# A fused attention, expert and mixing kernel: float32 projection weights split by one scaled pass on VectorE, and new order tables

## The chip, the cores and the metric

The kernel runs on one core of one Trainium2 chip. A core has five engines with queues of their own: TensorE (PE in the profile, its weight loads PEld), VectorE (DVE), ScalarE (ACT), GpSimd (POOL) and SyncE (SP), which here issues the DMAs. Each engine takes its instructions strictly in the order of its queue. The metric is the device time of one execution in microseconds, from the median of several runs.

## The reference, cut to what matters

Three stages follow one another on B = 2 batches of S = 768 rows. All arithmetic is float32.

```python
# 1. attention with 8 heads of 64; a key counts for a query only in the same hash bucket
q_bits = (einsum('bhsd,dk->bhsk', q, proj) > 0); k_bits = ...   # 6 bits each
scores = where(q_bucket == k_bucket, q @ k.T / 8, -1e9)
attn = softmax(scores) @ v
# 2. four causal attention experts, the best two of them weighted by a gate
logits = x @ w_gate; top 2; w = softmax of the two
for e in range(4):
    ye = causal_softmax((x @ wq[e]) @ (x @ wk[e]).T / 8) @ (x @ wv[e]) @ wo[e]
    out += w_e * ye
# 3. channel mixing with the row before
xk = mu_k * x + (1 - mu_k) * x_prev;  xr = mu_r * x + (1 - mu_r) * x_prev
out = sigmoid(xr @ w_r) * (relu(xk @ w_k) ** 2 @ w_v)
```

## The kernel before

The 1536 rows are twelve tiles of 128 (i = 0 to 11, six of each batch). A tile runs through three groups of steps: `lsh_steps` (per head h: `score`, a softmax, then `pv`, the product with the values), `moe_steps` (projections qk and v, per expert a causal softmax, the output projection o) and `mix_steps` (h, r and v: hidden layer, gate, down projection).

Nearly every matmul works on float16 pairs: a float32 array is split into a high part (`hi_part`, a scaled cast to float16) and a low part (`lo_part`, scaled value minus high part), and three products of the parts are summed. For a softmax this is a chain over all engines: the score matmul `s` on PE; on DVE one pass that scales and takes the minimum (P); on ACT the exponential; a high part on ACT or POOL and the low part on POOL (PHL); a DMA transpose from SP (PT); then `pv` on PE. The sixteen heads of tiles 0 and 1 (`F32T`) go another way: PE transposes the float32 P (tp), ACT or DVE copies it (PF), and `pv` is a float32 matmul, so POOL has no part in them.

The weights of stage 2 come in eight pieces through `split_w`: four of `WQK` (queries and keys), two of `WVG` (values and gate) and two of `WO`. Each piece is loaded into a float32 tile `w32` (named w_qk, w_v and w_o in the profile), multiplied in place by its scale (`nc.gpsimd.tensor_scalar`), cast to its high part, and its low part is made by `lo_part("p", ...)` on POOL. The weights of stage 3 come through `split_d` and are not touched.

The code does not issue instructions as it reads. It records operations (class `Program`; all of them then carry line 226 in the profile), and three tables at the end set what happens: `ORDER` is one order over all operations, from which every engine's queue follows, `HOMES` assigns buffers, and `ENGINES` may move a high part or a copy to ACT, DVE or POOL, whatever the letter in its call says. So "a" in `hi_part("a", ...)` is only a default: in this kernel ENGINES puts six of the eight weight high parts on POOL and two on ACT, and of the eight scalings in place seven on POOL and one on ACT.

Of the kernel before, what the change touches and what calls it, by code (L numbers as in the profile page):

```python
# [1001 lines left out]
cH5fY0kM_<TO4|IZJAvF^AV=a#uuuA0B-m%3E`xgQ9FU@+YClU#2%&CQ_kZV1%$wftn4&9$<QZn@jwR=BjjwomSdLkd3>3i=;@rF)1m{Z_s2WBY&nFj(zk`E)*x&*>}q
HEslC@Y&r>|G=mB8(l^}8}9hQZj&qN|MhqMTDRG)fQr7dp97ctWk1DDbz9tc*y`4~tNx02(AoXuhq(2wik}PD{0o1}zxOMlliTKA`rE#a|Jm2|LtS}(=(jt8$9^i*^Eu
rUzr#K96JVCx=@>rxU2Y;wg5B<%n+Nk@0i1Ui+$XOv4W`3Icgf{)4gD%;=PtVj{=0ANfAa{9Ji!(ByT9r_`)1x?GQ9Fr;Hz)$zxdQR17<=KKi#c{Z~hN|%{BEN0ABl%@
QaTKqhLM!?f>+n;e&tR#=tCy1lL^}j0|b<FTV}a;|;d~Ho_W6hudL?-gIl>mWu#UU<dr_XSkW}t<QjOe0$g1kA-p2!e_*OzP0b;-}#*oAQNta&2ZcG^)3A_=<hRQE8p2
ig{-&`w!i@2*6)Tpu8Z3W?R*yO=DYZ=J{vBAb&v!1z;Y<<2Kw&4hi~tD`nzs1EP<TZ#%IS4elOf}z5F1b3-`fNhz5^vKSYNDxC~yogOD5ZU|uYU`LGbifHK$|%VG<R39
%p!l*8E2(HFz=m>&z{WM2U*;$T0-AA<YtF}B3G5D$vuP~QrlVF`SK!+a+n9}YkzEP^F*wj1t8_yq7ApJHV!iiaT!q=BC>A&m4#AUl*o)Ew|Lj`CUIwL1#gpfw(YoNydQ
`xlrVGQcZ*iAmr!{)#m*EhK{zFvh2Y(wGQ-!8Ujj#`?DS9dkiqsD(A~KYW98+*~)48eo0Q2wff0FRmH>z;5nWH__*Y<d6v(;v3fpiQYO#<NY{4!F#HWnPC>iqbk@K&q9
1k0qrm)B!%|a0iU@uz%<EM#nX@q9y*{?&;*;}pLh;t(*>B~XZUG;j-T$Q`nkRu&hzIXALNC(R2@@89n24TV79M|&)r2xK+!27{e_7r2L0sb&^(Gsm!KXNfUEGcd*KQ~A
t((0;!J-XBGBLX(misY@UeU1x?pE40ukvgcEr2z)Lnz3Pz>f%DYyY2up|i0@=6P+6W)Y(cncO%akveODKSOxA8`>S4n|#Z8NJ8fummijGSCgX<6?gq7W&e#oUT9*?1`V  # L1010
TEZl=?@DDEXOZ-wwP355~^uoS)m8wH;?1vAa3RHll{&$S%|G*UV1<OH2_==I}le<Qd{4&4XNA{6vg^xl5F&4$9r%(eb!B0>bwrN}IgWoVJ9j9k-A5Ktz9DqqEP&7J6QT
#)A1fSg?jOu@eleB_bK|8xnU)*z8NiX0roTsm@IkbSdl$2URYdAo0C?)NpZ|)R*cNeG)+<~@mnhw%SNJh!29jy1{FVZUd7j6*yR3!cqZS?E>2A_t~QaVZ)(o+U{0=sFG
-$GkyFs`GFGz>TUthB|?#NoKr*MUrwh35O4^a}oRL+}u(Hy`{?9f}orJ-voAl$qW@O~^sNz&1KeM`#3&#8FrqM&lm(6~^E#T1`3WovQ`e=x;X;_tHLk3-6#VWT!^Z7#8
>s?xXw1t)Zhd1^;!I={?kg-=GQn=l0VEdO%HKEltJx&;T03c3SCwhl>0MG=ux}h~B%6G#_W-D!<yV@xQr0VXfam?csMf4L6b34zQCx!XNHWHy$_B2lxwq{6F*$=`nSLP
B5HjV+Go-onbn*<OR48|IeOB|2G_?+eG?=p3($dgt_PnRil4k3x0yL^aUnjUaCmBsS@3xyVM2l(f@(PuHY~~J)_T1fV#mqC`fbgITfNG(29SevG^78P*Hk8Gq5|f=DD~
SC*do4N%L?iBIcvXSd0qOa%{&ZxB-8M4m^T?rjcBn2$x|K{tqhCuhgF3(h@8|C8;Bqrq@)4R^Uopg^@7|uEr`<olf!^T**-}8vaIa=nwjn{-R&#A6kp+a3h}LQq+duQA
2LT8*l-arN$f`SMhuLoz~+fY;EOeGyYB6{AzAZHRuC1=k0!nZ^0Y53U9@oej{(kN?e(@;a+UY`>+}B#HzFhcj+#_+n1-x@-Nk<9k?H>@;a`@d;DI%kZV$P{zmJ$6Ys(r
# [23 lines left out]
HOMES = """
c-lQwjhdr443q5qL9*=Z!d$22XlZxbdH**&r8B+q@j;0rTe2MB`<IObEes%o(ToA6??xxns3&4^SA@gON7mWkP_&}-1V{Kl{)YV`e~?8Rfe8E~K=KXvm-a!0+KKo{|4T
c9750Zk5Set#CctJGya?Tsq9c_%`!m;I_yI2c-Cu=|#1IgO>W-7cd|uOu+j--=SH%TnWJbXkkwNxO)RDZuc(30?3!S)XOT+>8p*p_tqt>;V2n{&u59)rr_<n!bZdH_fS
#Qc?g~c;M8Q4;zWwDAOGI>H3+yZ>~t8NOm1r(=<<LIi$AM4#7ZB=EuE!m<X8e+w$%%O;=Ww`Y3HM5QtLmE)&rx&RBpt(RH$t}Rk*opS9dChiMCZ*Xhak8VGMBZAjLYj1
u63SS}I#e<z<S201YA+?AK4p)n5lrY!l9t%Je$%JjEl&$JNnO>U8Iv~D1|QW}^)2PZ+Pbr%Tw)Pp8F7)`-FMI0DK%PAP7xGvju_PYT?^c=55r|!eesLGo9ih_o{CiA!n
WS7?zhCKhL1HN)gmp_3w!#yJK8pTrW&-+O%QXWjY)nl_;mHoUsRQ|>paR8u2?xxk}uQkER2gyHv5Fl4t+Kta<wR*<cj0hKIWF63k($x`t=)FuuU#)($%dBQ8n?g9v-;f
n?3w$ZigEWyV}>a6T^&d6m1{mm}r$_u1v~zv-{5fVfz3D0lVx1oAu$ky`O#B&UV#Y{k-Oj=M9Y#F82{H@^qH9l15?BWkEAu0w%vVehswlB)@5kX4yNPVutCeCEL>l(`>
xkigv%9ebJDi51G(Mofj!&4xP3@8P$(6^h2cWU%>o6F<SAesOTZOD-x?xVr}WdWp1*Q+2?%7yxsay5~WII8+A5>q%=bx-_rfdtn=#K=GDGxXLqZ|FuGDJQ4xGI4e6{VF
PHOzW%$K6YCir0M^hcx
"""  # L1050
# [48 lines left out]
```

## Time and profile before

| | |
|---|---|
| median of 3 runs | 453.33 us (451.66 to 453.76) |
| profiled execution | 452.1 us |
| its span, first to last instruction | 450.3 us |
| mean granted TensorE clock | 0.996 |
| busy: PE, DVE, POOL, ACT | 433.4, 340.4, 321.9, 314.6 us |

The profile is one execution. The working of the prediction is made against its 452.1 us (span 450.3, and 1.8 around it); the median of the runs is 1.2 us above it. PE's busy time is that of pipelined records: a matmul that stands in the array while the next one waits for data counts as busy. So the busy share of PE overstates how much it does, and the chain of work that ended last is the better view of who holds the time in a stretch.

### The profile page before, as it was taken

How to read it: one execution, taken by the hardware profiler on the slowest of the kernel's cores; microseconds unless marked ns; L12 is line 12 of the kernel's file. 1: busy time of each engine (PE TensorE's matmuls, PEld its weight loads, DVE VectorE, ACT ScalarE, POOL GpSimd, SP SyncE). 2: the span in 40 equal slices, each digit the busy share in tenths (PEclk: the TensorE clock that was granted, in tenths of full speed). 3: DMA queues.
4: the chain of work that ended last, by engine and by line, in shares of the span. 5: the costliest groups of instructions: out<-in, count | busy, mean ns of one | idle time of the engine just before them, and what ended most of it. 6: DMA issues, size and time to landing. Idle time of an engine off the chain costs nothing.

```text
span 450.3 us, 14758 instructions
## 1 busy us (share of the span) xinstructions
PE 433.4 (96%) x6009; PEld 340.8 (76%) x6009; DVE 340.4 (76%) x914; ACT 314.6 (70%) x508; POOL 321.9 (71%) x345
## 2 busy tenths in 40 slices
PE   3999999999999999997999999999999999999997
PEld 3788988877888667687768876779679768966774
DVE  3899998999989878887877887578679676564431
ACT  5899899999796878885879575847757635550230
POOL 6915559789899958979879859799777847285020
PEclk9899999999999999999999999999999999999999
DMA  8987578999999997799979996999988975328101
GB/s 253 279 234 190 171 182 162 173 181 208 188 190 200 240 194 178 119 181 201 158 129 182 175 157 127 198 155 169 140 144 149 185 124 114 77 49 153 29 33 47
DMA packets 213428, 72.28 MB, mean 161 GB/s; under 512 B 204776, under 2 KB 209136, under 8 KB 213360
## 3 DMA queue, kind: packets, MB, share of 16 engines
q1 hardware_dynamic: 213184, 71.33, 83.4%
q8 instruction: 47, 0.77, 0.7%
q14 instruction: 21, 0.17, 0.1%
q10 hardware_dynamic: 176, 0.01, 0.0%
HBM read 22.04 MB, written 3.15 MB: 56 GB/s over the span
## 4 chain that ended last, share of the span: by engine, by line
PE 74%; POOL 9%; ACT 5%; DVE 5%; DMA 4%; issue 3%; POOLq 0%; ACTq 0%; DVEq 0%
PE x L226 12%; PE v L226 12%; PE h L226 12%; PE s L226 11%; PE qk L226 6%; PE r L226 6%; POOL PHL_m L226 4%; PE se L226 3%; PE o L226 3%; PE tp L226 2%; DMA PT_m<-PHL_m 2%; PE vg L226 2%; PE y L226 2%; ACT P L226 2%; POOL PHL L226 1%
## 5 line engine op out<-in xcount | busy, mean ns | idle before, releaser
L226 POOL TENSOR_TENSOR PHL<-P,PHL 128x768 f16<-128x768 f32 x80 | 134.0, 1686 | 16.7 <-ACT PHL L226 12.1
L226 ACT ACTIVATE P<-P,mx 128x768 f32<-128x768 f32 x96 | 88.0, 930 | 16.6 <-DVE P L226 14.4
L226 DVE TENSOR_SCALAR_CACHE_REDUCE P<-s 128x768 f32<-128x768 f32 x96 | 90.4, 950 | 10.4 <-PE s L226 5.2
L226 PE MATMUL s<-y,x 128*128 128x384 f16 x384 | 77.0, 328 | 0.8 <-DVE P L226 0.8
L226 PE MATMUL h<-mk,WK 128*128 128x128 f16 x1152 | 73.0, 219 | 0.1
L226 PEld LDWEIGHTS <-WK 128*128 128x128 f16 x1152 | 67.0, 98 | 4.6 <-issue 1.0
L226 PE MATMUL v<-WV,k2h 128*128 128x512 f16 (+1 forms) x208 | 57.7, 363 | 0.0
L226 PEld LDWEIGHTS <-x 128*128 128x128 f16 x480 | 38.6, 98 | 21.7 <-ACT x L226 3.3
L226 PEld LDWEIGHTS <-PT 128*128 128x128 f16 x1440 | 50.1, 98 | 5.9 <-issue 1.5
L226 PE MATMUL x<-vh,PT 128*128 128x65 f16 x960 | 53.4, 194 | 0.5 <-DVE xT L226 0.5
L226 PE MATMUL x<-vl,PT 128*128 128x64 f16 x480 | 39.4, 193 | 0.0
L226 POOL TENSOR_SCALAR PHL<-P 128x768 f16<-128x768 f32 x39 | 33.1, 851 | 8.3 <-ACT P L226 5.2
L226 POOL TENSOR_TENSOR PHL_m<-P_m,PHL_m 128x512 f16<-128x512 f32 (+2 forms) x24 | 33.8, 1415 | 6.6 <-ACT PHL_m L226 5.8
L226 PE MATMUL v<-WV,k2l 128*128 128x512 f16 (+1 forms) x104 | 37.7, 363 | 0.0
L226 PE MATMUL qk<-xT,WQK 128*128 128x128 f16 x576 | 37.0, 219 | 0.0
L226 ACT ACTIVATE PHL<-P 128x768 f16<-128x768 f32 x41 | 34.3, 838 | 2.3 <-PE x L226 0.7
L226 PEld LDWEIGHTS <-WQK 128*128 128x128 f16 x576 | 34.1, 98 | 2.0
L226 PE MATMUL r<-WR,mr 128*128 128x512 f16 x144 | 35.0, 379 | 0.0
L226 ACT ACTIVATE t<-h 128x512 f32<-128x512 f32 x24 | 14.2, 592 | 23.5 <-PE h L226 20.3
L226 PEld LDWEIGHTS <-k2h 128*128 128x128 f16 x208 | 18.6, 98 | 13.9 <-issue 1.0
L226 DVE SCALAR_TENSOR_TENSOR h<-h,t 128x512 f32<-128x512 f32 x24 | 16.6, 692 | 15.5 <-ACT t L226 15.5
L226 POOL TENSOR_TENSOR mk<-m32k,mk 128x512 f16<-128x512 f32 x12 | 14.2, 1185 | 17.6 <-ACT mk L226 15.9
(181 smaller groups left out, 929.5 us busy)
## 6 DMA issues: line engine op xcount, KB each, us to landing
raw_k<-in_moe_w_k_dram SPq DMA_DIRECT2D x8, 512.0 KB, 5.1
raw_v<-in_moe_w_v_dram SPq DMA_DIRECT2D x8, 512.0 KB, 4.5
q<-in_q_dram SPq DMA_DIRECT2D x12, 256.0 KB, 6.1
k<-in_k_dram SPq DMA_DIRECT2D x8, 384.0 KB, 4.2
v<-in_v_dram SPq DMA_DIRECT2D x8, 384.0 KB, 5.4
out_dram<-e SPq DMA_DIRECT2D x11, 256.0 KB, 2.7
raw_r<-in_moe_w_r_dram SPq DMA_DIRECT2D x4, 512.0 KB, 4.1
PT<-PHL SPq DMA_TRANSPOSE x80, 4.4
```

Source lines behind the costliest of these rows:

```text
L226: getattr(getattr(self.nc, engine), method)(*[real(a) for a in args], **{k: real(a) for k, a in kw.items()})
```

## The change

In `split_w` the scaling in place goes. The high part takes the scale itself, and the low part is one DVE instruction (scale times source minus high part) in place of a POOL subtraction. That is 8 scalings fewer, and 8 low parts that stand on DVE and no longer on POOL. `F32T` is as it was. All three tables are new.

```diff
-        nc.gpsimd.tensor_scalar(w32, w32, sc, 1.0, op0=OP.mult, op1=OP.mult)
-        hi_part("a", hi, w32)
-        lo_part("p", lo, w32, hi)
+        hi_part("a", hi, w32, sc)
+        lo_part("v", lo, w32, hi, sc)
...
 ORDER = """
-c-jrtg8~@F768%R>y2&Owr$(CZQHhO+qP}CK^v4w8#eF##F?q!)H&y!ICH_F0~g8Vb}?K8SKr5Vd0bvs)8%soTs#-wC2>_<85hM>a}iy2SJ35m30xsp*d=mhT~wFUC3d
+c-jrtg8~@F5&*#6yVb?EZQHhO+qP}nwr$(C(}rzQhHdlSe8m7L2vh)r0Fi)z0U<YdNC=Uk4CH~lP!_5}K8ONapga_Sa!?RzKm^DS4&p*Js1B7ODpY|TSP=@rH0Tb|pb`
...
```

The new ENGINES table also moves other high parts and copies. Counted over the program: off DVE go 4 PF, 6 copies of transposed queries (x), 2 kT, 2 qT, one each of WK, WR, WV, xT, y, yT and x2t, and three small zl; onto it come 3 vnh. Off ACT go 2 nak, 2 naq, 2 nbq, 3 vh, 2 mk, 2 hl_y, 3 vnh, a WQK and the one scaling that stood there, and it takes what left DVE besides 3 nbk. POOL takes 2 nak, 2 naq, 2 nbq, 3 vh, 2 mk, 2 hl_y and a WQK, and gives 3 nbk and a PHL_m. After the change the eight weight high parts stand on POOL (seven) and ACT (one, a WO).

Three places show the new order; behind P, s and PHL the first number is the head, behind q and nbq<-q the tile. The first is POOL's queue early in the program, behind the high part of query tile 1 (nbq<-q_1), where the first weight pieces are handled. Before:

```order
L226 TENSOR_SCALAR nbq<-q_1_238 128x8x64
L226 TENSOR_SCALAR w_qk_224<-w_qk_224 128x512
L226 MEMSET vh_0_284 128x24x2
L226 MEMSET causal 128x128
L226 AFFINE_SELECT causal<-causal 128x128
L226 TENSOR_SCALAR w_qk_332<-w_qk_332 128x512
L226 TENSOR_SCALAR WQK<-w_qk_332 128x4x128
L226 TENSOR_SCALAR WQK<-w_qk_224 128x4x128
L226 TENSOR_TENSOR WQK<-w_qk_224,WQK 128x4x128
L226 TENSOR_TENSOR WQK<-w_qk_332,WQK 128x4x128
L226 TENSOR_SCALAR nbq<-q_2_502 128x8x64
```

And the same place now:

```order
L226 TENSOR_SCALAR nbq<-q_1_148 128x8x64
L226 TENSOR_SCALAR nbk_0_1_96<-k_0_0_1_132 128x12x64
L226 TENSOR_SCALAR WQK<-w_qk_214 128x4x128
L226 MEMSET vh_1_365 128x24x2
L226 TENSOR_SCALAR nbk_0_0_200<-k_0_0_0_113 128x12x64
L226 TENSOR_SCALAR vh_0_98<-v_0_0_1_392 128x12x64
L226 TENSOR_SCALAR vh_1_365<-v_0_1_1_412 128x12x64
L226 MEMSET vnh_496 128x24x2
L226 TENSOR_SCALAR nbq<-q_2_432 128x8x64
```

Between the two query tiles POOL has one weight high part left of six weight passes, and two high parts of values (vh) have come in.

The second place is DVE's queue among the score passes (P) of tiles 0 and 1. Before:

```order
L226 TENSOR_SCALAR P_2_554,mx_391<-s_2_530 128x768
L226 TENSOR_SCALAR P_0_556,mx_391<-s_0_547 128x768
L226 SCALAR_TENSOR_TENSOR wd_k_0_552<-raw_k_0_399,wd_k_0_552 128x512
L226 TENSOR_SCALAR P_3_607,mx_608<-s_3_581 128x768
L226 SCALAR_TENSOR_TENSOR nbq<-q_2_502,nbq 128x8x64
L226 SCALAR_TENSOR_TENSOR WK_0_0_604<-wd_k_0_552,WK_0_0_604 128x512
```

And now, in front of the same low part of query tile 2 (nbq<-q_2):

```order
L226 TENSOR_SCALAR P_1_549,mx_390<-s_1_514 128x768
L226 SCALAR_TENSOR_TENSOR WK_2_512_553<-wd_k_512_536,WK_2_512_553 128x512
L226 TENSOR_SCALAR P_1_567,mx_568<-s_1_540 128x768
L226 SCALAR_TENSOR_TENSOR WQK<-w_qk_168,WQK 128x4x128
L226 SCALAR_TENSOR_TENSOR nbq<-q_2_432,nbq 128x8x64
L226 TENSOR_SCALAR P_2_600,mx_390<-s_2_561 128x768
```

A weight low part (WQK) now stands between score passes on DVE; it is the second of the eight, and six of them stand ahead of DVE's last score pass of tile 2.

The third place is POOL's queue among the PHL passes of tile 2, where the first piece of WO was handled. Before:

```order
L226 TENSOR_SCALAR PHL_2_1088<-P_2_983 128x768
L226 TENSOR_TENSOR PHL_2_1088<-P_2_983,PHL_2_1088 128x768
L226 TENSOR_SCALAR w_o_718<-w_o_718 128x512
L226 TENSOR_SCALAR PHL_5_1094<-P_5_905 128x768
L226 TENSOR_TENSOR PHL_5_1094<-P_5_905,PHL_5_1094 128x768
L226 TENSOR_SCALAR naq_1179<-q_9_771 128x8x64
L226 TENSOR_SCALAR WO<-w_o_718 128x512
L226 TENSOR_TENSOR WO<-w_o_718,WO 128x512
L226 TENSOR_TENSOR PHL_0_1141<-P_0_1121,PHL_0_1141 128x768
```

And now:

```order
L226 TENSOR_TENSOR PHL_1_1161<-P_1_1049,PHL_1_1161 128x768
L226 TENSOR_SCALAR PHL_7_1247<-P_7_1078 128x768
L226 TENSOR_TENSOR PHL_7_1247<-P_7_1078,PHL_7_1247 128x768
L226 TENSOR_TENSOR PHL_6_1153<-P_6_1103,PHL_6_1153 128x768
L226 TENSOR_SCALAR nbq_1254<-q_9_918 128x8x64
L226 TENSOR_TENSOR PHL_4_1210<-P_4_1130,PHL_4_1210 128x768
L226 TENSOR_SCALAR nbq<-q_4_926 128x8x64
L226 TENSOR_TENSOR PHL_5_1230<-P_5_1213,PHL_5_1230 128x768
```

No weight pass stands between these PHL passes any more; the one WO pass that POOL keeps comes ten instructions later, and high parts of queries (nbq) have come in.

## Rows read from the trace of the kernel before

**Rows 1.** Page, part 1: busy us, share and instructions by engine.

```profile
PE 433.4 (96%) x6009; PEld 340.8 (76%) x6009; DVE 340.4 (76%) x914; ACT 314.6 (70%) x508; POOL 321.9 (71%) x345
```

**Rows 2.** Busy time by stretch; each engine's busy us (instructions) stand in the header's order.

```profile
core 0: us, PE busy (x) PEld busy (x) DVE busy (x) ACT busy (x) POOL busy (x), PEclk, DMA share, GB/s
0.00:25.00 25.00, 17.08 (x206) 14.32 (x207) 15.85 (x41) 17.88 (x31) 18.62 (x34) 0.93 0.96 265
25.00:62.00 37.00, 37.00 (x348) 33.42 (x346) 35.54 (x75) 34.79 (x70) 15.22 (x16) 1.00 0.73 189
62.00:125.00 63.00, 60.70 (x923) 51.15 (x921) 58.70 (x175) 58.26 (x105) 55.91 (x58) 1.00 1.01 183
125.00:240.00 115.00, 111.55 (x1648) 84.37 (x1645) 96.28 (x247) 91.97 (x140) 97.03 (x97) 1.00 1.00 181
240.00:450.00 210.00, 207.03 (x2901) 157.54 (x2898) 134.06 (x379) 111.69 (x166) 135.10 (x142) 1.00 0.72 126
```

**Rows 3.** Chain that ended last, 25 to 62 us, shares by line.

```profile
by line: PE x L226 42.6%; PE s L226 24.6%; PE tp L226 21.3%; PE qk L226 5.4%; PE tr_x L226 4.8%; PE tr_y L226 0.9%; PE z_q L226 0.5%
```

**Rows 4.** The same chain, 62 to 125 us.

```profile
by line: PE x L226 17.5%; PE s L226 13.9%; POOL PHL L226 10.4%; DMA PT<-PHL 7.8%; PE qk L226 7.6%; PE tp L226 4.7%; PE h L226 4.4%; DVE P L226 3.9%; PE tr_x L226 3.7%; PE se L226 3.0%; PE vg L226 2.2%; PE o L226 2.2%; DVE xT L226 1.9%; POOL
```

**Rows 5.** Groups: PHL and the weight passes on POOL; count | busy us, mean ns | idle before.

```profile
L226 POOL TENSOR_TENSOR PHL<-P,PHL 128x768 f16<-128x768 f32 x80 | 134.0, 1686 | 16.7 <-ACT PHL L226 12.1 <-DVE y L226 1.4 <-DVE qT L226 1.1
...
L226 POOL TENSOR_TENSOR WQK<-w_qk,WQK 128x512 f16<-128x512 f32 x4 | 4.6, 1161 | 1.5 <-ACT WQK L226 1.3
...
L226 POOL TENSOR_TENSOR WVG<-w_v,WVG 128x512 f16<-128x512 f32 (+1 forms) x2 | 2.4, 1180 | 0.1
L226 POOL TENSOR_SCALAR w_qk<-w_qk 128x512 f32<-128x512 f32 x3 | 2.4, 786 | 6.4 <-DMA w_qk<-in_moe_wq_dram 6.4
L226 POOL TENSOR_TENSOR WO<-w_o,WO 128x512 f16<-128x512 f32 x2 | 2.3, 1162 | 1.5 <-ACT WO L226 1.4
...
L226 POOL TENSOR_SCALAR w_v<-w_v 128x512 f32<-128x512 f32 (+1 forms) x2 | 1.2, 625 | 0.5 <-DMA raw_k<-in_moe_w_k_dram 0.5
...
L226 POOL TENSOR_SCALAR w_o<-w_o 128x512 f32<-128x512 f32 x2 | 1.2, 620 | 0.0
```

**Rows 6.** Waits of POOL, 25 to 62 us: total us, times, longest.

```profile
POOL w_qk L226 <- DMA w_qk<-in_moe_wq_dram: 6.4, 1, 6.4
POOL WQK L226 <- ACT w_qk L226: 5.4, 1, 5.4
```

**Rows 7.** DVE low parts nbq with two operands in SBUF: ns min/median/max, first and last start.

```profile
L226 DVE SCALAR_TENSOR_TENSOR nbq<-q,nbq x8: 682/760/1179, 5.5 to 206.0; 128x512 f16<-128x512 f32 x8
```

**Rows 8.** Timeline: DVE low parts and the POOL passes beside them; start us, us.

```profile
16.95 0.69 DVE L226 SCALAR_TENSOR_TENSOR nbq<-q,nbq 128x512 f16<-128x512 f32 x1 [1.05 <-POOL nbq L226]
16.99 1.12 POOL L226 TENSOR_SCALAR w_qk<-w_qk 128x512 f32<-128x512 f32 x1
...
86.40 1.09 DVE L226 SCALAR_TENSOR_TENSOR nbq<-q,nbq 128x512 f16<-128x512 f32 x1
86.97 2.02 POOL L226 TENSOR_TENSOR PHL<-P,PHL 128x768 f16<-128x768 f32 x1
```

**Rows 9.** Groups that ENGINES moves: count | busy us, mean ns | idle before.

```profile
L226 ACT ACTIVATE PF<-tp 128x384 f32<-128x384 f32 x24 | 11.2, 495 | 0.3 <-PE tp L226 0.3
L226 ACT ACTIVATE x<-tr_x 128x512 f16<-128x512 f16 x15 | 8.4, 589 | 2.0 <-PE tr_x L226 1.8 <-DVE x L226 0.2
L226 DVE COPY x<-tr_x 128x512 f16<-128x512 f16 x17 | 6.6, 415 | 0.4 <-POOL mk L226 0.4
L226 DVE TENSOR_SCALAR PF<-tp 128x384 f32<-128x384 f32 x8 | 4.4, 552 | 0.6 <-PE tp L226 0.6
L226 ACT ACTIVATE vh<-v 128x768 f16<-128x768 f32 x5 | 4.2, 839 | 0.2 <-DMA v<-in_v_dram 0.2
L226 POOL TENSOR_SCALAR nak<-k 128x768 f16<-128x768 f32 x4 | 4.1, 1023 | 2.2 <-DMA k<-in_k_dram 1.9
L226 ACT ACTIVATE nak<-k 128x768 f16<-128x768 f32 x4 | 3.4, 839 | 2.3 <-DMA k<-in_k_dram 1.7 <-DMA PT_m<-PHL_m 0.6
```

More of the change, by code (lines that the diff above doesn't have):

```diff
@@ L1002 @@
[L1002 to L1017, printed above, removed]
@@ new lines @@
+UySkG<VJOo$0E5k|nHPzfvJC;W`1@Cv5DtJv2i!~X6A4uRwt3uE94NbJ``N*oR`F*fFcaZnOh!Uiaf{ain2YS;0LT*90<z+J}37!mJd6g-6+VI&NNj~EG8L3Y>#1#z;Q
+;*P;)nCc$kSeFqW<7yZN<6IeB18d;{zQSMeA)dw?coxsV8JqxL@Lzn5$DtFf)pOVmZsJXU0;aj!INnWncW{P#ga6?VyoD3oM0XMfx}Whqe#IpIH#`NC+*x>nm*8*w1qZ
+p)FcAj3Z}=A1xp(*-pW>hRJ3hm|a58`!4}airm)s}y=U{|O=Kn$O&cjHz+`YsUeu%pOL*06}!9B;z@DpByneGK%0dgzcN|(|vaH;$#sDf94-7JT0m`m-eVl@<Z4V+u$(
+)u)h4$OA#VU!!~()rq$!PmkXILFO}g-%_1zsOyOj6Rbe<L1F)m)Y0Ejc${B0;}D8Sf`s^9ju4ug3IFTVtt(JZuvE?h+hB=aG7h3^V|}b)o1e!v8XTRyTC$-;O4u=*cm%
@@ new lines @@
+RJG||mLL+Q~O)-jVhR>i2w!z4*Jw|uM{RVA|-EghzfZcJ6YmPbmbJ*%i_^!CkwZM*;&-cLXt|i8BFW?^J_dRh6G_&0<r;q4%xJa&mkLseid%mE*<CnTZ{;tpNce$M|iM
+#L9xCj0vOod!Nw@>aK`lN1;d*oBNy{;3+bm`q=pVr-nukyraaJ?{&OXgC#eXf+x<72ssz7_Vt-Wbo7_UT-F_tYnFsa#j+hkfz6FXK!4O1>K;bT52tSJ}sPqp^n1=q6Go
+SKn9h{jq{?>L)=WHvp^pXMVqH;19Tg*wEMXg?&9=)_?RjU=SX3ljv_h7|Z!uehA)zPyVR833+{W-^|~JL$0~M1E2kG{)nsX-}<|7*d24JT~?RbWpi0vBR>=y`)WS1JK-
+Kcc30lN^Cw*n*TjGK(Wr%g2szzIJnnM2I{v+{>%aJ~emIW6==2C0+c5ma|L(ubuRgbH<sChSQTWYIrGNZnYU%U1K%U0nG|KBD&>y~y|KR`hQ|P59`qxjvvG|jZNaOL8n
+}Dr-TmQ4q=l=4q{5ZVo?z(n<Dz^92@U)wZ)2V}>K^=WTHxbXenKX-LQvvs%|KaD+9QqCJxlVpQz4nD%es|u@r3<czn}iqL4R_5Ic1%JKTv1ov6?0`>IcF4u-uN@FxQjy
@@ new lines @@
+$Bhl{=lS;TUuB5x<fOb%1nvLh&ER0H*-A<Z`f54w`-92>o-6OZ3{(_rs4#uLtp_J?FOS=P9f{_+bH@}PK;(Uxt^Kb#~rmnt=KT8Lxr*GsMxcV+0b@%Zp3hklCu9t7<ln
+4*ea%}8+_!StN5>ON8@f<BA#&@s`pSXYImb>j1(Mn82$LKKq0|{vvohQMjZZTb;i=<e=C8i~G$2D`u=@(dqt1$^BrAqEStf6F7#U-aTc!Ew+Ww)Gug%q?FhxzGP)qQ|!
+?jwA3z5R2Sl8(??s^QkrQ}@hWaWC8qtnT{xm+lm8qSW-0``Nv6uiXHjmM&3Emx|KRUK;4v>mXl}-?;Vk)~%plTspc%OKCIx3#TaqRdgFDBMtU_{7;aceswFUzaQea(0|
+a^{{X;MG{%qh@7+eaLGRo|KgoY^*J&Xx!o@h<BmU+l`>izGucmQ+hTlfp=_cK#J2cbx=etzPEx{6$iAMO^u8#Za{&chaQvB@xa6iLF%}Rf{-`y9Noj$=gSJ%CQdhRIgq
@@ L1039 @@
+%x4=9R`Mbwm=`t6X_NDgi2P7Pugv}Z|AIUxMO#1Sa>SWWRX_3e&K;Vv`01~3<`t8xbWD9hw-6Zcw$xTsdWs`taIoeMurJtRH$lQLZ?v8x`rWPVrU;0>k?h69YVM8K|V_
+NuuOlG-{lYaQ>xo@8xVf77xvN$S|MAmE3}xc)W76!S*4%kXB!=QgfU@gcx|h-h)oK=+t^Ul-q?Ga5(?Wpn-)G=X)9yJZE7fCC9Razu$orO%Gz7|#U_X8;WztWGs3SnGt
+3IJ!)GaHbHX21-fEi<e_I{<Y=7A&qwuGFv9I>cFu3sj|H)XRbHn_wFf0xdG|USN!lJMwSXdL5g%Bcyr6FQi5$ak!t8Z&Vq_8}!4lBdD5IOu~tHS>9uN@2xY<>98HiRE`
+AnXkL0)#_hQ`i``gw0`V*cP^jBVk849HNA%AzFwYVuW2`cQ_i3h2!BwI2lfb)8R}w8!m)BVQ)AW8ru1AF<c6l!<BF~TnpF3jc_yk4@ABGj{
 """
@@ L1046 @@
[L1046 to L1049, printed above, removed]
+c-lo&4R@O`5If!Z3)_UPX~Q7tl9Y}9|9?1Ln!dpckY}GP>12yMuc!kcxj-TQGc6K)Kt-X(7eYxe3;Z&z(4;=f*_<l^1pa|G!B5x^VF`-xfmgAC6+jhv1Ad8pi2N1(4b8
@@ L1055 @@
-D{we^^r8-(xPaWi?XHwu7sjr3CjU!
+c-pO12@=F02$SUhf8KF>d4K~b)6z~W5FlbHov<oAFN*NFUO`>YsxCWBHYlADmHYl_MLjFhXy@Vsg5jAK-ZgLB$@#q1xO#28y`#noRYNNk^FVhp?yxWtl6n(l=m8C)Ow9
+_^86Rvc0MiVtvPV`aat*sAV9%6*+p##eFiw(Wn2OhD%)w|>kBvioL$&jYF*b|6XO^RkcIza?IMG{|+pwZD&c`-xj0u=a8A9TsYV6#T5NU&R5DQbL4nzFyL`ju%T;wRh=
+vZbDwq@%W`P>;PdHDf8j{%$
 """
```

62 lines of the change are left out of this document (31 added, 31 removed).

## The prediction

> **What bounds the kernel now.** I read the page's first part, then busy time by stretch, then the chain of work that ended last in each stretch, and only then single groups. By the first part TensorE is busy 433.4 of 450.3 us [rows 1], but that counts matmuls that stand waiting in the array, so the chain decides who holds the time. The stretches [rows 2] show four phases. From 0 to 25 us everything fills up: PE is busy 17.08 us, the granted clock is 0.93 on the mean, DVE, ACT and POOL have 15.85, 17.88 and 18.62. From 25 to 62 us, the float32 heads, the chain is PE alone [rows 3], yet DVE (35.54 of 37.00) and ACT (34.79) are nearly full beside it, while POOL has 15.22 and is mostly idle. From 62 to 125 us all are nearly full (DVE 58.70, ACT 58.26, POOL 55.91 of 63.00) and the chain jumps: POOL's PHL passes hold 10.4% of it, the transposes behind them 7.8%, DVE's score passes 3.9% [rows 4]. From 240 us PE has 207.03 of 210 while DVE has 134.06, ACT 111.69 and POOL 135.10: there the other engines wait for PE and nothing that the change does to them counts, unless it is moved there in bulk. So the change can win or lose between 0 and 240 us, and which engine is relieved matters only by stretch.
>
> **GpSimd's side: 14.1 us of passes go.** Low parts: 4.6 (WQK), 2.4 (WVG), 2.3 (WO); scalings in place: 2.4, 1.2, 1.2 [rows 5]; sum 14.1 us. Of this, WQK and WVG (10.6 us) lie between 17 and 50 us. From 25 to 62 us POOL stood idle for 21.8 us [rows 2], 6.4 of it waiting for the w_qk load and 5.4 for the one scaling that ACT did [rows 6], and the chain has no POOL piece there [rows 3]. Those 10.6 us are worth nothing by themselves. The WO passes, 2.3 + 1.2 = 3.5 us, and the 1.4 us for which POOL waited for ACT's WO part [rows 5], 4.9 us in all, lie in the full stretch. POOL holds there 10.4% of a chain of 63 us, 6.5 us, in its PHL passes [rows 4]; a pass less ahead of them is time only where POOL's queue, and not the exponential ahead of it, was last. Bounds: 0 and -4.9. I take -1.0, near the zero end, since the new table puts seven or eight high parts (nak, nbq, naq, vh) into POOL's queue, at 1.02 us for a nak [rows 9], so POOL's relief over the program is nearer 9 than 14 us.
>
> **VectorE's side: eight passes come.** Each is 512 columns from two operands in SBUF. The trace has no such pass on w32, but its nearest kin is the low part of the queries: same shape, same two operands in SBUF, 682 to 1179 ns, median 760 [rows 7]. Eight of them are 5.5 to 9.4 us. Six stand early, where POOL is mostly idle, so I take 0.70 for these; two (WO) stand among PHL passes, and I take 1.09 [rows 8]: 4.2 + 2.2 = 6.4 us. What leaves DVE by the tables: 4 PF at 552 and 6 copies at 415 ns [rows 9], 4.7 us; eleven others less three vnh that come, net eight at about 0.5 us as an estimate from these two rows, 4 us. Over the program DVE is some 2 us lighter. But the eight passes are all in front of 125 us, and where DVE had 1.46 us to spare from 25 to 62 us and 4.3 us from 62 to 125 us [rows 2], six early ones (4.2 us) do not fit without something leaving. Some does: the copies and PF of the float32 heads lie in this same stretch. I count what stands ahead in the tables' order at two landmarks, every instruction at its group's mean, an estimate. At DVE's last score pass of tile 5 DVE has about 2.8 us more ahead of it than before, and PE about 4.8 us more; at that of tile 8, both have about 3 us less. So the tables moved PE's work along with DVE's, and the lead of DVE over PE grows by about 1 us at its worst place. Bounds: 0 (all covered by what left) and +4 (six passes uncovered). I take +1.0.
>
> **The port that both engines use.** The row at 86.40 us shows the DVE pass at 1.09 us in place of 0.69, and POOL's pass beside it at 2.02 [rows 8] in place of 1686 ns on the mean [rows 5]; at 16.95 us DVE kept 0.69 and POOL's scaling of w_qk took 1.12 [rows 8], where 0.62 is the time of the w_v scaling [rows 5]. The Trainium skill, page "SBUF — State Buffer", section "Who interferes with whom", states that a VectorE instruction with two SBUF inputs contends with a GpSimd instruction that reads SBUF, and that the loser is fully blocked. Both rows agree with it as far as a loser goes, but the losses are 0.4 to 0.5 us, not the 1.65 us of a whole PHL pass. By the rule each of the eight passes would cost one engine up to such a wait; it speaks against the change and is priced among the rivals.
>
> **ScalarE's side.** It takes the 4 PF at 495 and the 6 copies at 589 ns, 5.5 us, and some eleven others, and gives 2 nak and 3 vh at 839 ns, 4.2 us [rows 9], and about a dozen small ones. The net is near +3 us over the program, an estimate from these rows. Between 25 and 125 us ACT was busy 34.79 + 58.26 = 93.05 of 100 us [rows 2], so what comes early can push the exponentials back. Bounds 0 (PE's work moved along, as at the landmarks above) and +2.5 (most of it early and uncovered); I take +0.5.
>
> **Start, buffers, transfers, end.** The load order at the start puts the key halves of heads 4 to 7 first and one half behind a weight block. The first score pass, which needs those heads, could come earlier; but PE's queue holds the transposes of the late half ahead of it, and the bytes in front of the last key half are the same as before. I take 0, bounds -1.5 and +1.5. The number of transposes and loads is the same, and the DMA share of 1.01 and 1.00 from 62 to 240 us [rows 2] gets no relief: 0. Behind 240 us PE's work is the same, instruction for instruction, and I take -0.5 for 62 to 240 us as a whole, where the tables carry about as much work as before but POOL's queue is some 9 us less far behind; bounds -3 and +3.
>
> **Sum.** -1.0 + 1.0 + 0.5 + 0 - 0.5 = 0. Against the profiled execution that is 452.1 us; the median of the runs is 1.2 us above it, and since the profile is one execution inside a range of 451.66 to 453.76 us I put the forecast between the two, at 452.6 us. A measurement of this kernel can tell about 0.5%, 2.3 us, from no change.
>
> **The rivals.** First, faster: POOL's queue is what holds the chain from 62 to 240 us more than the exponentials are, and the relief reaches PE. For it speaks the 10.4% of POOL in the chain, against it that POOL waited in that same stretch for ACT. Price: the 4.9 us of WO, or 3.9 with 1.0 already counted, and up to 1 to 2 us at the start: 452.6 - 4 = 448.6, at best 447. Second, slower: DVE becomes the bound between 25 and 125 us. It decides from the point at which more than the spare 1.46 us (25 to 62) is added net of what leaves; then every further us of DVE delays the score passes, the exponentials behind them, and PE's pv. Price: six early passes, 4.2 us, less 1.46, is 2.7, and ACT's 2.5 on top: 452.6 + 5 = 457.6. Third, each of the eight passes meets a POOL pass that reads SBUF, as at 86.40 us: DVE's cost goes to 8 x 1.18 = 9.4 us, 3.0 above the 6.4 counted, and where POOL loses its PHL passes grow by 0.35 us: 452.6 + 3 = 455.6. For it speaks the row at 86.40 us, against it that six passes stand where POOL is busy 15.22 of 37 us. It adds to the second. (This is how it would go by the rule of the Trainium skill's page "SBUF — State Buffer" cited above.) Fourth, the change does not do what it says on ScalarE: its high parts are put on POOL by the table (seven of eight), so ScalarE has nothing to gain; that is in the sum already and gives the forecast.
>
> **How the numbers follow.** No change that can be measured, 450.3 to 454.9 us: 0.40. Faster by the relief of POOL: 0.33. Slower by DVE or by the port, 0.27, of which 0.07 is the port alone. For the range I leave out 1 in 10 on either side: a third of the faster cases lies below the 4 us that the WO passes are worth, and a third of the slower ones above the 5 us of DVE and ACT, so 447.5 to 458.0. The likeliest case's own range is the 450.3 to 454.9 above.
>
> **What would show it.** Right: eight SCALAR_TENSOR_TENSOR on WQK, WVG and WO at 0.69 to 1.1 us on DVE; POOL's busy time down by about 9 us and DVE's by 1 to 3; DVE at 35 to 37 of 37 us and the chain still PE alone from 25 to 62 us; the stretch from 240 us unchanged. Wrong towards slower: PE idle or DVE in the chain between 25 and 62 us, the last score pass of tile 1 later by over 2 us. Wrong towards faster: POOL's PHL below 8% of the chain from 62 to 125 us and PE reaching the same matmul 3 us earlier at 125 us. The forecast fails as a whole if the tables change the coupling of the queues at places that no row here names, since a new order over all operations is more than the eight passes that I could price.

## The result

| kernel | us, median (lowest to highest) | ratio to before, 95% interval |
|---|---|---|
| before | 452.67 (451.66 to 453.76, 4 runs) | 1 |
| after | 447.19 (447.05 to 448.11, 4 runs) | 0.988 (0.985 to 0.991) |
| after, measured again beside later experiments | 447.48 (446.85 to 449.04, 6 runs) | 0.992 (0.989 to 0.995) |

The change makes the kernel 4 to 5 us faster. The forecast was 452.6 us, no change, with 447.5 as the low end of its range: wrong. The profiled execution of after took 448.11 us, with a span of 446.3.

### The profile page after: what moved, and what is told of

Same layout as the page of the kernel before. It is cut to its first block, busy times and chain, and to the rows that moved or that the text cites. A ratio compares the mean times of both kernels' runs of the same rounds, so it can differ in the third digit from the quotient of the medians.

```text
span 446.3 us, 14743 instructions
## 1 busy us (share of the span) xinstructions
PE 430.6 (97%) x6009; PEld 339.2 (76%) x6009; DVE 336.3 (75%) x901; ACT 317.1 (71%) x518; POOL 315.3 (71%) x340
## 4 chain that ended last, share of the span: by engine, by line
PE 62%; ACT 11%; POOL 9%; DVE 9%; DMA 4%; issue 4%; SPq 0%; POOLq 0%; DVEq 0%; ACTq 0%
PE v L226 11%; PE h L226 11%; PE x L226 8%; PE s L226 8%; PE r L226 6%; POOL PHL L226 5%; PE qk L226 4%; ACT P L226 3%; PE o L226 3%; DVE P L226 3%; PE y L226 2%; PE se L226 2%; PE vg L226 2%; POOL PHL_m L226 2%; DMA k<-in_k_dram 2%
## 5 line engine op out<-in xcount | busy, mean ns | idle before, releaser
L226 POOL TENSOR_TENSOR PHL_m<-P_m,PHL_m 128x512 f16<-128x512 f32 (+2 forms) x24 | 34.7, 1450 | 7.6 <-ACT PHL_m L226 6.8
L226 ACT ACTIVATE P_m<-P_m,bias_m 128x512 f32<-128x512 f32 (+2 forms) x24 | 19.6, 821 | 20.5 <-DVE P_m L226 17.9
L226 DVE SCALAR_TENSOR_TENSOR h<-h,t 128x512 f32<-128x512 f32 x24 | 16.6, 694 | 19.8 <-ACT t L226 19.7
```

Of the source, the lines that this page charges most:

```text
L226: getattr(getattr(self.nc, engine), method)(*[real(a) for a in args], **{k: real(a) for k, a in kw.items()})
```

## The profile after

Part 1 of the page of after (busy us, share, instructions; [rows 1] before):

```profile
PE 430.6 (97%) x6009; PEld 339.2 (76%) x6009; DVE 336.3 (75%) x901; ACT 317.1 (71%) x518; POOL 315.3 (71%) x340
```

POOL is 6.6 us lighter, DVE 4.1 lighter, ACT 2.5 heavier. By stretch, beside [rows 2], same columns:

```profile
0.00:25.00 25.00, 16.19 (x207) 13.39 (x208) 16.62 (x40) 18.35 (x33) 15.49 (x31) 1.00 0.99 278
25.00:62.00 37.00, 37.00 (x326) 32.84 (x324) 33.54 (x75) 36.54 (x78) 13.51 (x15) 1.00 0.75 170
62.00:125.00 63.00, 61.28 (x971) 52.16 (x969) 59.94 (x173) 57.83 (x107) 58.16 (x57) 1.00 0.99 191
125.00:240.00 115.00, 113.18 (x1714) 87.95 (x1711) 98.78 (x249) 92.79 (x138) 98.61 (x100) 1.00 0.98 186
240.00:450.00 210.00, 202.99 (x2810) 152.90 (x2806) 127.46 (x367) 111.61 (x167) 129.57 (x139) 0.99 0.69 122
```

From 25 to 62 us DVE is 2.0 us lighter, although passes on the weights were added: more left it there than came. ACT is 1.75 us heavier and has 0.46 us left. From 62 to 125 us POOL is 2.25 us **heavier**: the tables put more into its queue there than the weights took out. The chain of 62 to 125 us shows who is late there ([rows 4] before: POOL PHL 10.4%):

```profile
by line: POOL PHL L226 20.3%; issue 12.5%; DVE P L226 11.9%; ACT P L226 7.5%; POOL nbq L226 3.0%; DVE m32k L226 2.7%; POOL gt L226 2.6%; ACT P_m_p L226 2.6%; ACT PHL L226 2.6%; DVE P_m_p L226 2.5%; DVE rs L226 2.5%; ACT PF L226 2.4%; DVE m3
```

and that of 25 to 62 us, which was PE alone in [rows 3]:

```profile
by line: PE x L226 24.7%; PE s L226 19.8%; ACT P L226 19.3%; PE tp L226 14.9%; ACT PF L226 6.7%; ACT raw_r L226 3.1%; PE tr_x L226 3.0%; DVE P L226 2.6%; ACT wd_r L226 1.4%; ACT WO L226 1.4%; ACT WK L226 1.3%; ACT WR L226 1.3%; PE tr_y L226
```

The eight new passes (ns min/median/max; first and last start):

```profile
L226 DVE SCALAR_TENSOR_TENSOR WQK<-w_qk,WQK x4: 683/698/1210, 18.1 to 50.6; 128x512 f16<-128x512 f32 x4
...
L226 DVE SCALAR_TENSOR_TENSOR WVG<-w_v,WVG x2: 790/854/919, 61.6 to 67.4; 128x528 f16<-128x528 f32 x1, 128x512 f16<-128x512 f32 x1
...
L226 DVE SCALAR_TENSOR_TENSOR WO<-w_o,WO x2: 1099/1414/1730, 88.7 to 95.0; 128x512 f16<-128x512 f32 x2
```

Together 3.3 + 1.7 + 2.8 = 7.8 us. They stand later than the prediction had them: both WVG passes are at or behind 62 us.

**PE's lag** is the measure for where time goes: the time at which a matmul starts, less what all the matmuls ahead of it on PE take back to back (worked out from the step between matmuls of each shape in these traces; 414.9 us in all, the same in every kernel). It is read at equal amounts of PE work, since the orders differ:

| PE work done, us | 24 | 48 | 64 | 88 | 104 | 184 | 192 | 240 | end |
|---|---|---|---|---|---|---|---|---|---|
| before | 13.5 | 13.4 | 15.0 | 17.0 | 19.5 | 24.5 | 26.9 | 28.7 | 32.0 |
| after | 13.4 | 13.5 | 14.4 | 17.3 | 18.5 | 22.2 | 22.2 | 24.3 | 28.0 |
| new passes, old order | 13.6 | 16.2 | 18.6 | 20.8 | 23.5 | 28.7 | 29.6 | 31.3 | 34.6 |
| old passes, new order | 13.6 | 13.7 | 14.7 | 19.8 | 21.0 | 23.5 | 23.5 | 25.6 | 29.2 |
| new order, WO old | 12.8 | 12.9 | 13.8 | 19.0 | 20.2 | 23.0 | 23.0 | 25.0 | 28.6 |
| new order, only WO new | 13.4 | 13.5 | 14.5 | 17.4 | 18.5 | 21.1 | 21.2 | 23.2 | 26.8 |
| old order, only WO new | 13.4 | 13.2 | 15.6 | 17.8 | 20.5 | 25.7 | 30.0 | 31.7 | 35.0 |
| before, early query turn | 13.1 | 13.0 | 14.6 | 16.7 | 19.1 | 24.2 | 24.5 | 26.6 | 29.9 |

A row is one execution, and those of one kernel differ by 1 to 2 us (after, profiled again: 13.7 at 24, 16.3 at 64, 29.0 at the end). In that case most of it comes where the granted clock differs. Here is the stretch from 70 to 78 us in after and in after again (columns as in [rows 2]):

```profile
70.00:78.00 8.00, 7.23 (x90) 6.51 (x90) 7.86 (x19) 7.48 (x14) 6.83 (x6) 1.00 1.16 217
70.00:78.00 8.00, 7.23 (x74) 6.83 (x74) 6.36 (x15) 6.58 (x10) 6.14 (x5) 0.79 1.24 213
```

PE is busy for the same 7.23 us in both, but has 74 matmuls instead of 90 where part of the stretch ran at the lower of the clock's two levels, 1.2 instead of 2.4 GHz. The row "old order, only WO new" is affected too: it is an execution of 455.14 us (median of that kernel 453.1), with a granted clock of 0.79 on the mean from 212 to 220 us, in the stretch in which its lag rises from 25.7 to 30.0.

Between before and after nothing happens in the first 48 us of work. One us is gained by 104, 1.3 more on the way to 184, then 2.4 at once between 184 and 192, and nothing behind that.

The sudden step is a stall of the kernel before, in its timeline at 203 to 213 us (start us, us, [idle before <-releaser]):

```profile
203.57 1.23 SPq L226 DMA_TRANSPOSE x<-naq  x1
...
210.35 0.60 ACT L226 ACTIVATE t<-h 128x512 f32<-128x512 f32 x1 [2.91 <-DMA x<-naq]
...
212.34 0.58 ACT L226 ACTIVATE x<-tr_x 128x512 f16<-128x512 f16 x1
...
212.97 0.36 PE L226 MATMUL z_q<-prhl,x 128*128 128x12 f16 x8 [2.04 <-ACT x L226]
```

HOMES gives `t` of tile 3 the slot in which `naq` of tile 8 lay, and SP issued the transpose that reads `naq` only at 203.57, in its queue behind other transfers. ACT waited 2.9 us for it, the copy of `x` stood behind `t` in ACT's queue, and PE's hash of tile 7 behind that. In the tables of after the two do not meet. The weights have no part in it. How much it costs varies: with the new passes in the old order the lag rises by only 0.9 us there, from 28.7 to 29.6.

## Experiments

**The theory**: the gain belongs to the order of the work (A), in part to that one stall. **Rivals**: GpSimd's relief itself (B); the passes cost VectorE time that the order wins back (C). The further letters (A1, A2, D, E, F) are defined in the expectations that use them. Differences in microseconds are the ratio's distance from 1, times 452 us, unless something else is named; the runs stem from four chips, and each was measured beside before on its own chip.

### Passes and tables apart

```diff
 split_w as after (no scaling, low part on VectorE)
-ORDER, HOMES, ENGINES of after
+ORDER, HOMES, ENGINES of before, without the eight scalings
```

> The new way of splitting the weights (scale and round in one pass, one VectorE pass for the low part) in the order, the slots and the engines of the kernel before; the eight scalings are dropped and each low part stands where its GpSimd pass stood. Theory A (the gain is the order of the work, not the passes): 452 to 453 us, as before, and ScalarE still waits 2.9 us for the transpose of the queries at 207 to 210 us, with the 2.0 us stall of PE behind it. Theory B (GpSimd's relief is the gain): 447 to 449 us, as after. Theory C (the eight passes on VectorE cost, and the order had to win that back): 454 to 457 us.

Measured: 455.35 us, 1.007 of before (1.005 to 1.010): 3.2 us slower. C's size, and B is out for this order.

```diff
 ORDER, HOMES, ENGINES of after, each scaling put ahead of its high part
-split_w as after
+split_w as before (scaling and low part on GpSimd)
```

> The other corner: the order, slots and engines of the kernel after, but the weights split as before: eight scalings on GpSimd, each right in front of its high part, and eight low parts on GpSimd. Theory A (order): 447 to 449 us, at most 1.5 us above the kernel after. Theory B (relief of GpSimd): 451 us or more, since the 14 us of passes are back in GpSimd's queue. No stall of ScalarE at about 207 to 210 us by either, since the slots are those of after.

Measured: 449.53 us, 0.993 (0.990 to 0.996): 3.2 us faster than before without any new pass, some 2 us short of after. So the tables alone win about 3 us, and **the same passes cost 3.2 us in the old order and save 0.5 to 2 us in the new one** (0.993 against the two measurements of after, 0.988 and 0.992; with the second the intervals overlap, so the saving rests on the waits shown under the WO pieces as well).

In the old order DVE's queue around 40 us shows the cost:

```profile
39.30 0.95 DVE L226 SCALAR_TENSOR_TENSOR WQK<-w_qk,WQK 128x512 f16<-128x512 f32 x1
40.18 1.09 DVE L226 SCALAR_TENSOR_TENSOR WVG<-w_v,WVG 128x512 f16<-128x512 f32 x1
...
41.31 0.67 DVE L226 TENSOR_SCALAR rs<-sm 128x4 f32<-128x4 f32 x1
...
42.70 0.41 DVE L226 TENSOR_TENSOR x<-x,rs 128x256 f32<-128x256 f32 x1
```

and the waits of that kernel from 38 to 47 us what PE paid (total us, times, longest):

```profile
PE tp L226 <- DVE nbq L226: 0.9, 1, 0.9
...
PE x L226 <- DVE x L226: 0.7, 1, 0.7
```

Two passes stand ahead of `rs` and `x` of tile 0, for which PE waits: 2.8 us of lag by 48 us of work (16.2 against 13.4). In after they stand behind score passes (at 30.57 and 43.45 us), and PE loses nothing there.

The two halves of the tables, the order (with the slots) and the engines, were then split:

```diff
 kernel after
-ENGINES of after
+ENGINES of before for 182 operations (the weights' stay)
```

> The kernel after with the 182 operations that its engine table moved put back on the engines of the kernel before (the weights' passes stay as in after, and so do order and slots). Theory A1 (what makes room for the eight passes is the move of copies from VectorE to ScalarE): VectorE is about 2 us busier early, PE loses 1 to 3 us before 62 us of its work, 449 to 452 us. Theory A2 (where the instructions stand in the order is what counts, the engines little): 446.5 to 448.5 us.

Measured: 502.92 us, 1.113.

```diff
 new passes, ORDER and HOMES of before
-ENGINES of before
+ENGINES of after
```

> The new split of the weights and the engines of the kernel after, but the order and slots of the kernel before. Beside the run with the old engines as well (455.4 us). Theory A1 (engines make room): the 2.2 us that PE loses at 41 to 43 us there go, 450 to 453 us. Theory A2 (places count): 454 us or more, since the two passes on WQK and WVG still stand ahead of rs and x of tile 0, on which PE waits.

Measured: 498.47 us, 1.106. In the first run both theories missed by 50 us; in the second A1 missed by 45, and A2 had named no upper end. The waits of the first show queues out of step (the same two lines are 12.1 and 20.3 us in all in before):

```profile
POOL PHL L226 <- ACT PHL L226: 37.5, 14, 8.2
ACT t L226 <- PE h L226: 28.2, 13, 9.7
```

An instruction that changes its engine without changing its place stands in a queue that was not ordered for it, and whatever is behind it waits; that this is the whole of the 50 us is argued from these waits, not shown. Order and engines cannot be taken apart here, so how much each gives stays open.

### The stall at the end of the gain

```diff
 kernel before, SP's queue
+DMA_TRANSPOSE x2_8<-naq_8
 DMA_TRANSPOSE PT_m5_1<-PHL_m5_1
 dma_start v32_1_0_1
-DMA_TRANSPOSE x2_8<-naq_8
```

> The kernel before with one instruction moved: the transposing DMA of tile 8's queries goes three places earlier on SP's queue, right behind the first PT_m of tile 5, so that the slot which ScalarE's t of tile 3 takes over is free in time. Theory A (this one stall is worth 2.2 to 2.4 us of the 5.5): 450.2 to 450.6 us, and the lag of PE does not jump at z_q7. If something else is late next at the same place: 452 to 453 us. If the earlier transpose delays the PT_m behind it on the queue: above 453 us.

Measured: 450.2 us, 0.997 (0.995 to 0.999): 1.5 us faster, and the lag goes from 24.2 to 24.5 where before goes from 24.5 to 26.9. The stall is real and worth 1.5 of the 4 to 5 us (0.5 to 2.4 by the interval). (The transpose moved ahead of the two transfers shown, one place less than its expectation says.)

### The WO pieces

```diff
 kernel after
-all eight pieces split in the new way
+WQK and WVG in the new way, the two WO pieces as before
```

> The kernel after, with the two WO pieces alone split as before (scaling and low part on GpSimd, about 4 us of passes in the full stretch from 62 to 125 us); WQK and WVG as in after. With all eight pieces split as before in this order it was 449.5 us. Theory A (the relief of GpSimd counts at WO alone, -2.5 us): 449 to 450 us, with the loss at s_4 and y_1 at 103 to 107 us. Rival (the relief of the early pieces counts as well): 447.5 to 448.5 us.

Measured: 448.87 us, 0.995 (0.992 to 0.998). That is, within the intervals, the time with all eight pieces as before (449.53, 0.993): in this order the WO pieces seem to carry all that the new passes save. The interval also overlaps that of after's second measurement (0.989 to 0.995), so the trace has to decide. Where, the timeline of this kernel shows from 98 to 104 us, first POOL, then who waits for it:

```profile
98.41 1.16 POOL L226 TENSOR_TENSOR WO<-w_o,WO 128x512 f16<-128x512 f32 x1
...
99.53 2.10 POOL L226 TENSOR_TENSOR PHL<-P,PHL 128x768 f16<-128x768 f32 x1
...
101.67 0.96 DVE L226 TENSOR_SCALAR_CACHE_REDUCE P<-s 128x768 f32<-128x768 f32 x1 [1.54 <-POOL PHL L226]
...
103.40 0.60 ACT L226 ACTIVATE WR<-wd_r 128x512 f16<-128x512 f32 x1 [2.56 <-DVE rs L226]
```

In after, the same DVE pass:

```profile
102.48 0.96 DVE L226 TENSOR_SCALAR_CACHE_REDUCE P<-s 128x768 f32<-128x768 f32 x1 [0.50 <-POOL PHL L226]
```

In the new order POOL runs without a gap here, and a score pass needs the slot that POOL's low part still reads. The wait reaches PE; its waits in this kernel from 98 to 107 us:

```profile
PE y L226 <- DVE WR L226: 1.7, 1, 1.7
PE s L226 <- DVE P L226: 0.8, 1, 0.8
```

With all eight pieces as before they are 1.6 and 0.8 us; in both profiles of after, and with only the WO pieces new, the first is 0.6 us and the second is absent. Here POOL **is** last, and a pass less in its queue is time: the lag at 88 us of work is 19.0 with the old WO pieces and 17.3 without, at 104 us 20.2 and 18.5.

```diff
 kernel after
-all eight pieces split in the new way
+the two WO pieces in the new way, WQK and WVG as before
```

> The kernel after, with the six early pieces (WQK and WVG) split as before, on GpSimd, and only the two WO pieces split in the new way. Theory A (the WO pieces are the whole gain of the new passes; the six early ones cost VectorE what the prediction said, +1.0 us): 445.5 to 446.5 us, faster than after. Theory F (GpSimd's relief by the early pieces counts too, since its queue is behind from there on): 448 to 450 us.

Measured: 447.01 us, 0.991 (0.989 to 0.994), beside 447.48 for after on the same chip:

> The kernel after, unchanged, as a measure for the other three on the same chip: 446.5 to 447.5 us, 0.988 to 0.990 of before.

Both theories missed: the times are the same within the noise. So the six early pieces are worth nothing that these runs can tell in the new order, on either engine, and WO is what counts. In the old order:

```diff
 kernel before
-all eight pieces as before
+the two WO pieces in the new way, at the places of GpSimd's passes
```

> The kernel before, with the two WO pieces alone split in the new way (no scaling, low part on VectorE, at the places where GpSimd's passes stood); WQK and WVG as before. In the new order these two pieces were worth 2 to 3 us. Theory A (GpSimd's relief at WO counts in any order): 449 to 450.5 us. Theory E (in the old order VectorE's passes at 75 to 102 us cost what GpSimd's relief gives): 451.5 to 453 us.

Measured: 453.1 us, 1.005 (1.002 to 1.007): 2.1 us slower (by the medians on that chip, 453.1 and 451.7, 1.4), which is theory E. The same edit has the other sign. POOL's timeline of this kernel around 70 us:

```profile
68.16 0.62 POOL L226 TENSOR_SCALAR WO<-w_o 128x512 f16<-128x512 f32 x1
70.67 1.65 POOL L226 TENSOR_TENSOR PHL<-P,PHL 128x768 f16<-128x768 f32 x1 [1.89 <-ACT PHL L226]
```

and that of before:

```profile
69.86 1.16 POOL L226 TENSOR_TENSOR WO<-w_o,WO 128x512 f16<-128x512 f32 x1
70.97 1.65 POOL L226 TENSOR_TENSOR PHL<-P,PHL 128x768 f16<-128x768 f32 x1
```

POOL is done with WO 2.2 us earlier and then waits 1.89 us for ACT's high part: the PHL pass starts 0.3 us earlier, no more. In the old order ACT was last, and the relief turned into a wait. The 1.23 us that the pass takes on DVE stay, and PE's `vg` waits 0.6 us for the copy behind it. The second piece shows the same: POOL skips 1.16 us of WO and then waits for ACT:

```profile
99.29 1.64 POOL L226 TENSOR_TENSOR PHL_m_p<-P_m_p,PHL_m_p 128x512 f16<-128x512 f32 x1 [2.26 <-ACT PHL_m_p L226]
```

In before this pass starts at 98.76 us, in an execution that is 0.5 us ahead by then.

```diff
 kernel before, only WO new, DVE's queue
-low part of WO (first piece)
 PF of tile 1, vl, P_m_p, lg, zl_q3, z_q3
+low part of WO (first piece)
```

> The kernel before with the two WO pieces split in the new way (453.1 us, +2.1), and the first of their VectorE passes moved behind PF of tile 1, vl and the hash sum of tile 3, some 4 us later on VectorE. Theory A2 (the place of the pass): the 0.9 us that PE lost at vg_0 at 74 us go, 451.5 to 452.5 us. Theory D (VectorE's sum in this stretch): the loss comes back a few us later, 453 us or more.

Measured: 453.05 us, 1.005 (1.002 to 1.007): no gain. The 0.6 us wait went from `vg` at 74 us, and one of 0.8 us came up at `x` (tile 2) at 78.7 us. That is theory D's number, but not plainly its mechanism: the trace names a memset late in POOL's queue there, and no run takes that apart.

```diff
 kernel before
+the two WO pieces in the new way
+DMA_TRANSPOSE x2_8<-naq_8 two transfers earlier on SP, as above
```

> The kernel before with two edits by hand: the WO pieces split in the new way, and the transposing DMA of tile 8's queries three places earlier. The second alone gave 1.5 us. Theory A (the gain of after is these two things, each added to the other): 447 to 449 us, within 0.5% of the kernel after. Theory E: 450 us or more, and the rest of the gain is the new order as a whole.

Measured: 451.52 us, 1.000 (0.998 to 1.002). -1.5 and +2.1 nearly cancel. Theory A in this form (stall and WO relief, each by itself) falls: the WO relief is worth something only in an order in which POOL is last.

### The early pieces

```diff
 kernel after
 lo_part("v", lo, w32, hi, sc)
+lo_part("v", lo, w32, hi, sc)
```

> The kernel after with each of the eight low parts made twice on VectorE, the same result written again: about 7.9 us more of VectorE, all between 18 and 96 us. It measures the prediction's VectorE term. If VectorE is covered there (six passes beside PE's float32 heads), the time rises by less than 1 us. If the term was right in kind (VectorE is the bound as soon as 1.5 us is added net), it rises by 3 to 6 us.

Measured: 451.5 us, 0.998 (0.996 to 1.000), 4.0 us above after by the medians (447.48), 2.8 to 4.5 by the ratios. So a third to a half of the added 7.9 us of DVE reaches the end: DVE is covered by little there, and the tables had to make room for the first eight.

```diff
 new passes, order of before, DVE's queue
-low parts of one WQK and one WVG piece
 nbq, rs, wd_k, x, P, WK, P
+low parts of one WQK and one WVG piece
```

> The new split of the weights in the order of the kernel before, with two of the eight VectorE passes (one on WQK, one on WVG) moved behind the next three score passes and x of tile 0, so that rs and x are no longer behind them. Nothing else moves. Theory A2 (a pass costs by its place): the 1.9 us at tp0_0_2 and x_0_0 go and stay gone, 453 to 453.6 us. Theory D (VectorE's sum is the bound from 25 to 62 us): they come back a few us later at another instruction, 455 to 456 us.

Measured: 458.46 us, 1.014 (1.011 to 1.017): 3 us slower again, missed by both theories. `rs` and `x` were on time, but the low part also frees the slot for the next weight. SP's queue in this kernel, and then in before:

```profile
44.60 0.33 SPq L226 DMA_DIRECT2D w_o<-in_moe_wo_dram  x1
...
46.12 1.27 SPq L226 DMA_DIRECT2D raw_k<-in_moe_w_k_dram  x1
```

```profile
37.33 0.33 SPq L226 DMA_DIRECT2D w_o<-in_moe_wo_dram  x1
...
40.45 0.34 SPq L226 DMA_DIRECT2D raw_k<-in_moe_w_k_dram  x1
```

HOMES gives `w_o` the slot of that WQK piece. SP's waits of the kernel with the move, 34 to 50 us, name the pass:

```profile
SPq L226 <- DVE WQK L226: 7.5, 1, 7.5
```

It is 3.9 us without the move, and in before 1.3 us in two waits, there for POOL's WQK. The load waits for the slot and goes out 7.3 us later than in before (4.3 later than without the move), and behind it in SP's queue stand the loads of `q` and `raw_k`. ACT then waits for `raw_k`, with exponentials behind it in its own queue, and PE for these (waits of 40 to 56 us):

```profile
ACT raw_k L226 <- DMA raw_k<-in_moe_w_k_dram: 4.0, 1, 4.0
...
PE tp L226 <- ACT P L226: 3.1, 1, 3.1
```

```diff
 new passes, order of before, DVE's queue
+low parts of one WQK and one WVG piece
 zl_q2, z_q2, nbq
-low parts of one WQK and one WVG piece
 rs, x
```

> The new split in the order of the kernel before (455.4 us), with two of the VectorE passes (one on WQK, one on WVG) moved ahead instead of behind: right behind their high parts, ahead of the copy of z_q2. The load of w_o, which takes the slot that one of them frees, can then go out at about 38 us, as before, instead of 40.3 us. If a pass costs by what stands behind it (rs and x on VectorE, the slot and the loads on SP): 454 to 455 us, the load of w_o at 38 us, PE's loss at 41 to 43 us 1 to 1.5 us instead of 1.9 to 2.2. If VectorE's sum alone counts: 455.4 us as before the move.

Measured: 454.24 us, 1.006 (1.004 to 1.009). 0.5 us better than where they stood, within the interval: the time settles nothing. The trace bears out half of the expectation: PE's waits between 36 and 58 us sum to 0.6 us instead of 1.8, but `w_o` still goes out 3.9 us behind the `w_v` load ahead of it (4.5 without the move, 1.6 in before).

### The stalls that after still has

```diff
 kernel after, DVE's queue
-rs, reciprocal of tile 1
 P_2_4, z_q3, xT_0, nbq
+rs, reciprocal of tile 1
...
-P_7_4
 P_7_7
+P_7_4
```

> The kernel after with two short moves on VectorE: rs of tile 1 and its reciprocal go behind the marks of tile 3 (rs took 1.50 us at 69 us instead of 0.16, beside a GpSimd pass, and PE waited 0.8 us for the marks), and at 217 us the score pass of head 7 goes ahead of that of head 4, which waits 0.95 us for a slot that GpSimd still reads while PE waits for the other. If both stalls are PE's alone: 1.5 us faster than after, 445.3 to 446 us. If something else is late next at either place: 446.5 to 447.5 us.

Measured: 447.04 us, 0.990 (0.988 to 0.992). Both stalls of PE are gone from the trace, but `z_q8` at 229 us now waits 1.0 us, and the time is that of after.

```diff
 the same kernel, DVE's queue
+four m32 passes of tile 4
 P_7_5
```

> The kernel after with the two moves tried already (447.0 us, no gain) and a third: four m32 passes of tile 4 go ahead of the score pass of head 5 of tile 7, which waited 2.57 us there, so that the PSUM slot that z_q8 needs is free about 1 us earlier. If the stalls are worth their time once nothing is late behind them: 445 to 446 us. If the next one takes their place: 446.5 to 447.5 us.

Measured: 447.13 us, 0.991 (0.988 to 0.993). Again the time of after; the wait of `z_q8` only went from 1.0 to 0.8 us. What single waits of 0.9 us show was not there to be had in these two tries: something else is late right behind them.

## Why the prediction was wrong

**The step that failed is the one for the tables.** "I take -0.5 for 62 to 240 us as a whole", bounds -3 and +3, was an estimate from how much work the tables carry. The order alone gives -3.2 us, the low bound. About half of it is the stall at 210 us (1.5 us), which could have been found in the trace of before: PE idle for 2 us behind an ACT wait for a transpose of other work. I had looked for what the passes touch, and not for stalls that a new slot table might remove. With 0.5 to 2 us for the passes in the new order, the -3.2 give the measured 4 to 5 us. The faster rival had 448.6, at best 447, close to the 447.2 measured, but that is luck in the larger part: it put the whole gain on POOL's relief.

**GpSimd's relief, -1.0 with bounds 0 and -4.9: the kind was right, the order to judge it by was wrong.** For the old order I argued that POOL waits for ACT, so that little is gained; the run with only WO new shows just that (1.89 us of waiting, then a start 0.3 us earlier). But the forecast is for the new order, and there POOL is last: its share of the chain from 62 to 125 us did not fall below 8%, the sign I had named for the faster rival, it rose to 20.3%. It is the order that raised it: with the old passes in the new order PHL has 21.5% and the WO passes themselves 4.5%. The sign was the wrong way round: if the relieved engine leaves the chain, the relief has been used up; if it fills the chain, a pass taken out of its queue can count, as WO's did. Of the early pieces, 10.6 us on POOL, the prediction said that they are worth nothing by themselves, and that held.

**VectorE's eight passes, +1.0 with bounds 0 and +4.** At 7.8 us they cost more than the 6.4 counted, and in the old order all of it together (WO included) costs 3.2 us, near the upper bound. In the new order the six early ones cost nothing, by the run with them on GpSimd. What I took for likely happened: more work left DVE there than came, and it is at 33.54 us of 37 instead of the 35 to 37 forecast. Doubling the passes showed how thin the cover is.

**What my view of the early passes lacked** is the slot: a low part is also what frees `w32` for the next load. I had priced the pass by who waits for DVE, and "the number of transposes and loads is the same" as 0. When a load goes out, not how many there are, is what moved 3 us in the run with the two passes later.

**ScalarE, +0.5:** 2.5 us more work, as forecast (near +3), and its exponentials are 19.3% of the chain from 25 to 62 us, where [rows 3] had PE alone; the lag at 48 and 64 us of work shows no loss. **Start, and the stretch from 240 us:** 0, as forecast; the lag is the same up to 48 us of work, and the gap between the two kernels is 4.4 us at 240 us of work and 4.0 at the end. **The port:** right in kind and wrong in size, below.

**Busy time:** POOL -6.6 (forecast -9), DVE -4.1 (-1 to -3), ACT +2.5 (+3): the sums were forecast fairly, and said little about the time.

**What stays open:** the tables' other half, 1.7 us by the times and 1.0 us by the lag at 184 us of PE work, has no single place; order and engines could not be separated; and about 1 us goes with the granted clock, below.
